# Attention and ResMLP on one Trainium2 core: the third product of the last group added straight from PSUM, one store moved to ScalarE's queue, and a new written order

## The chip, the cores and the metric

The kernel runs on one core of one Trainium2 chip. The core has five instruction streams: TensorE (matrix products; PE in the profile, its weight loads PEld), VectorE (DVE), ScalarE (ACT), GpSimd (POOL) and SyncE (SP), which here issues only DMAs; ScalarE and GpSimd issue some as well. The metric is the device time of one launch in microseconds, the median of several runs.

## The reference

```python
kv  = einsum('bhsd,bhse->bhde', k, v)          # 8 batches, 8 heads, 576 rows, 64 per head
o   = einsum('bhsd,bhde->bhse', q, kv)
x   = o / sqrt(mean(o*o, -1) + 1e-6) * g_norm  # then (b, s, h*d): 8 x 576 x 512
tok = einsum('ts,bsd->btd', w_tok, alpha1 * x + beta1)
u   = x + lam * tok
ch  = maximum((alpha2 * u + beta2) @ w_ch1, 0) @ w_ch2      # 512 -> 2048 -> 512
out = u + lam * ch
```

All inputs and the output are float32.

## The kernel before

The kernel is written for a planner. The class `Prog` records every operation (a group of matmuls with one purpose, one arithmetic instruction, or one DMA) with a number in the order of creation, and what it reads and writes. A string, `ORDER`, then lists all these numbers in one global sequence. Each engine executes its own operations in just that sequence; nothing is reordered on the chip. In the string `751:4+807:0` means that the matmuls of 751 and 807 are woven into each other, 751 taking PSUM bank 4 and 807 bank 0; an operation that opens a bank waits for all users of that bank's tile before. `GATES` adds waits that no data asks for: `632: 652` makes 632 wait for 652. `synchronize` turns all this into semaphores.

**The work.** Each batch has 576 rows: four blocks of 128 and a tail of 64. Tails of two batches share one tile of 128 rows, `xt[:, 0]` or `xt[:, 1]`. For each batch `kv` (line 638) multiplies k and v; ScalarE copies half of the result (`kvo`, L655), VectorE adds it to the other half (`kvc`, L657). `load_kv` loads k and v of the next batch on GpSimd's queue: 1 MB each (L1465) and a small tail each (L1469). `qt_steady` turns q: a VectorE transpose (L1475) and a ScalarE copy (L1478). `norm` (L729) multiplies q by kv and normalizes (L696 to L717; L714 and L712 are the last multiplications on VectorE). `tok` (L812) mixes the rows and VectorE adds the result (L822). `a2_dma` casts it on GpSimd (L900) and transposes it by DMA on SyncE's queue (L913) to `a2m`, the input of the channel MLP.

**Channel MLP.** The first product is `ch1` (L1090) with a ReLU on ScalarE (L919), for the last two batches `pairmm` (L1031, with the kept sums L1043) and `tailmm` (L972, ScalarE's copies L982). The second product is done in the Strassen-Winograd form by `strassen(b)`: seven `product`s (L1212) of half size in three PSUM banks `ta`, `tb` and `tc`. Weight and row sums are made by `both` on VectorE (L1174). A bank that goes on accumulating while one of its partial sums is needed elsewhere is treated by `keep`: ScalarE copies the bank to `tmp` (L1242), GpSimd adds `tmp` to the result (L1245). A finished sum is added by VectorE straight from PSUM, `last_add` (L1250). `store` then writes rows out (L1259 for tails, L1263 else; L1341 and L1345 are the stores of `finish`).

`strassen(NB)` is the last group: the tails of batches 4 to 7, one quarter of the usual size. Its operations from the third product on, with their numbers before:

| operation | engine | what |
|---|---|---|
| 1565 | VectorE | last add of batch 7, 128x512 |
| 1589, 1590 | TensorE | third product into `tc` |
| 1591, 1592 | ScalarE, GpSimd | `keep(tc, (dn, fh))`: copy and add |
| 1593, 1594 | TensorE | product into `ta` |
| 1595 | VectorE | `last_add(ta, dn, fh)`, on the same rows as 1592 |
| 1596, 1597 | SyncE, ScalarE | stores of those rows |
| 1598, 1599 | TensorE | product into `tc`, which goes on |
| 1600 | VectorE | `last_add(tc, up, fh)` |
| 1601, 1602 | SyncE, SyncE | stores of those rows |
| 1603, 1604 | TensorE | last product, into `ta` |
| 1605 | VectorE | `last_add(ta, dn, fl)` |
| 1606, 1607 | SyncE, ScalarE | stores of those rows |

Other numbers that come up below: 629, 639, 1146 (VectorE, adds and multiplications), 652, 1196 (VectorE, weight and row sums), 1199 (VectorE, last add of a batch), 1203 (GpSimd, `keep`'s add), 1234 and 1236 (VectorE, transposes of q) with the copy 1235 (ScalarE), 1277 (VectorE, L714), 633, 637, 645, 987, 991, 995, 999 (SyncE, transposes L913), 558, 564, 905, 917 (SyncE, stores), 743 to 746 (GpSimd's k and v loads; 743 and 745 the large, 744 and 746 the small ones), 716 (TensorE, product), 751 (TensorE, `norm`), 807 (TensorE, `ch1`), 1282 (TensorE, `tok`), 1331 (ScalarE, ReLU), 1344 and 1350 (ScalarE, kept sums), 1467 and 1475 (TensorE, `tailmm`), 1555, 1556, 1576, 1577, 1585 (TensorE, products).

Of the kernel before, what the change touches and what calls it, by code (L numbers as in the profile page):

```python
# [10 lines left out]
ACT = mybir.ActivationFunctionType  # L11
# [92 lines left out]
"""  # L104

GATES = {23: 52, 38: 67, 39: 73, 40: 163, 124: 151, 125: 213, 204: 196, 233: 269, 234: 216, 235:
# [7 lines left out]


class Op:


    __slots__ = ("tile", "q", "kind", "cost", "lat", "fns", "idx", "deps", "raw", "alloc", "tiles", "at",
                 "pos", "waits", "inc", "clock", "slot", "nbytes", "ns", "val", "form", "bias")  # L120

    def __init__(self, q, kind, cost, lat, fns, pri, idx):
        self.q, self.kind, self.cost, self.lat = q, kind, cost, lat
        self.fns, self.idx, self.bias = fns, idx, pri
        self.deps, self.raw = set(), set()
# [233 lines left out]
def bass_transnormer_attn__then__resmlp_affine_kernel(  # L359
# [15 lines left out]
    with ExitStack() as stack:  # L375
        P = Prog(nc, stack)
# [842 lines left out]
        def strassen(b):  # L1219
# [58 lines left out]
            if tails:  # L1278
                store(0, fl)
# [343 lines left out]
```

## Time and profile before

| what | value |
|---|---|
| median of 3 runs | 327.81 us (327.43 to 328.18) |
| the profiled execution | 328.12 us |
| its span, first to last instruction | 326.3 us |
| TensorE busy | 319.0 us, 98% |
| VectorE, ScalarE, GpSimd busy | 250.2, 177.1, 141.9 us |
| granted TensorE clock | 1.000 |

Times in rows of the profile are microseconds from the start of the span. A row of the timeline has the start, the duration, the engine, the line in the kernel, the operation, what it writes and reads, its shape and the number of instructions put together; in brackets stands how long the engine was idle before it and what ended the wait. A row of the waits has the total, the number and the longest. SPq and ACTq are DMA issues on the queues of SyncE and ScalarE; a DMA's landing is told apart from its issue. PEld are weight loads, which run ahead of the matmuls that use them.

### The profile page before, as it was taken

Reading aid. Unit: us, or ns where it says so; the run is one execution under the profiler, and the core shown is the slowest. Engines: PE = TensorE matmul, PEld = TensorE weight load, DVE = VectorE, ACT = ScalarE, POOL = GpSimd, SP = SyncE. Lnnn points to the kernel's source line nnn. Section 1 sums busy time; section 2 is a strip of 40 time slices with the busy share of each in tenths; the row PEclk is TensorE's granted clock in tenths of the full one; section 3 lists DMA queues with packets and bytes.
Section 4 is the critical chain, followed back from the end, with each engine's and each line's share of the span. In section 5 each row is a group of like instructions: output and inputs, shape, how many; then the busy total and the mean of one; then the engine's idle time right before and its main releaser. Section 6 shows DMA issues by size and latency. Waiting matters only on the chain.

```text
span 326.3 us, 6145 instructions
## 1 busy us (share of the span) xinstructions
PE 319.0 (98%) x2411; PEld 218.2 (67%) x2441; DVE 250.2 (77%) x459; ACT 177.1 (54%) x363; POOL 141.9 (43%) x147
## 2 busy tenths in 40 slices
PE   8989999999999999999999999999999999999996
PEld 7767664454766545786579874787657644589884
DVE  4586078667799997838985388889899899997672
ACT  5684572329633471738741876731883068765520
POOL 3699127798362562353337143455234600014041
PEclk9999999999999999999999999999999999999999
DMA  7999997999950994799449950998040340000116
GB/s 258 316 267 257 214 243 176 224 151 209 265 123 16 204 245 70 173 247 217 104 50 186 259 104 11 213 253 171 2 129 2 64 145 4 0 2 2 64 50 209
DMA packets 108532, 48.15 MB, mean 148 GB/s; under 512 B 82061, under 2 KB 101717, under 8 KB 108504
## 3 DMA queue, kind: packets, MB, share of 16 engines
q0 software_dynamic: 26800, 21.38, 33.4%
q1 hardware_dynamic: 72240, 25.06, 33.4%
q10 hardware_dynamic: 9464, 1.32, 2.5%
q8 instruction: 19, 0.31, 0.4%
q14 instruction: 9, 0.07, 0.1%
HBM read 38.82 MB, written 9.44 MB: 148 GB/s over the span
## 4 chain that ended last, share of the span: by engine, by line
PE 91%; DMA 3%; DVE 2%; ACT 1%; issue 1%; POOL 0%; ACTq 0%; SPq 0%
PE ps L1090 25%; PE ps L1212 25%; PE ps L1151 10%; PE ps L812 9%; PE ps L1031 7%; PE ps L729 3%; DMA hh<-in_moe_w_tok_dram 2%; PE ps L638 2%; PE ps L1104 2%; PE ps L972 2%; PE ps L857 1%; DMA xm<-in_q_dram 1%; PE ps L594 1%; PE ps L644 1%; PE ps L877 1%
## 5 line engine op out<-in xcount | busy, mean ns | idle before, releaser
L1090 PE MATMUL ps<-a2m,w 128*128 128x512 bf16 x370 | 96.1, 384 | 0.5 <-DMA a2m<-a2b 0.3
L717 POOL TENSOR_TENSOR rm<-xm,la_bc 128x512 bf16<-128x512 f32 x28 | 35.3, 1272 | 60.7 <-DVE xm L714 43.6
L1090 PEld LDWEIGHTS ps<-a2m,w 128*128 128x128 bf16 x384 | 36.2, 97 | 37.4 <-DMA a2m<-a2b 0.5
L919 ACT ACTIVATE hh<-ps,b 128x512 bf16<-128x512 f32 x72 | 47.5, 687 | 18.6 <-PE ps L1090 13.3
L1245 POOL TENSOR_TENSOR xm<-xm,tmp 128x512 f32<-128x512 f32 x18 | 22.8, 1270 | 63.5 <-DVE qp L1174 28.6
L729 PE MATMUL ps<-kvc,qt 128*128 128x128 f32 (+1 forms) x140 | 42.3, 403 | 0.1
L1212 PE MATMUL ps<-w,hh 128*128 128x256 bf16 x344 | 41.8, 273 | 0.1
L1212 PEld LDWEIGHTS ps<-w,hh 128*128 128x128 bf16 x344 | 33.4, 98 | 6.1 <-issue 0.4
L1151 PE MATMUL ps<-w,hh 128*128 128x512 bf16 x138 | 36.9, 385 | 0.1
L638 PE MATMUL ps<-vr,kr 128*128 128x128 f32 x112 | 34.7, 409 | 0.0
L699 DVE TENSOR_REDUCE small<-sq 128x8 f32<-128x512 f32 (+1 forms) x35 | 23.4, 675 | 11.7 <-ACT sq L696 11.6
L812 PE MATMUL ps<-rm,wt 128*128 128x512 bf16 x107 | 29.0, 381 | 0.3 <-DVE rtl L712 0.2
L1250 DVE TENSOR_TENSOR xm<-ps,xm 128x512 f32<-128x512 f32 x24 | 16.3, 687 | 16.5 <-POOL xm L1245 8.9
L729 PEld LDWEIGHTS ps<-kvc,qt 128*128 128x128 f32 (+1 forms) x140 | 27.2, 195 | 2.3 <-DVE kvc L657 0.7
L900 POOL CAST a2b<-xm 128x512 bf16<-128x512 f32 x24 | 14.3, 612 | 32.6 <-DVE xm L822 20.1
L1478 ACT ACTIVATE qt<-qp 128x576 fp32r<-128x576 f32 x24 | 16.0, 680 | 16.0 <-DVE qp L1475 16.0
L707 DVE TENSOR_TENSOR ps<-ps,small 128x512 f32<-128x512 f32 (+1 forms) x35 | 24.2, 694 | 0.6
L1242 ACT ACTIVATE tmp<-ps 128x512 f32<-128x512 f32 (+1 forms) x21 | 11.8, 566 | 23.5 <-PE ps L1212 23.4
L696 ACT ACTIVATE sq<-ps 128x512 f32<-128x512 f32 (+1 forms) x35 | 20.6, 596 | 6.7 <-PE ps L729 6.3
L919 ACT ACTIVATE hh<-ps 128x512 bf16<-128x512 f32 x32 | 17.5, 596 | 12.1 <-issue 7.4
L638 PEld LDWEIGHTS ps<-vr,kr 128*128 128x128 f32 x112 | 22.4, 200 | 1.5
L1151 PEld LDWEIGHTS ps<-w,hh 128*128 128x128 bf16 x144 | 13.4, 97 | 13.5 <-issue 0.4
(216 smaller groups left out, 616.8 us busy)
## 6 DMA issues: line engine op xcount, KB each, us to landing
out_dram<-xm SPq DMA_DIRECT2D x32, 256.0 KB, 2.4
kr<-in_k_dram POOLq DMA_DIRECT2D x7, 1024.0 KB, 8.0
vr<-in_v_dram POOLq DMA_DIRECT2D x7, 1024.0 KB, 8.2
qs<-in_q_dram SPq DMA_DIRECT2D x20, 288.0 KB, 4.4
w<-in_moe_w_ch_dram POOLq DMA_DIRECT2D x8, 512.0 KB, 10.9
xm<-in_q_dram SPq DMA_DIRECT2D x8, 288.0 KB, 5.8
qs<-in_v_dram SPq DMA_DIRECT2D x4, 288.0 KB, 5.7
w<-in_k_dram SPq DMA_DIRECT2D x4, 288.0 KB, 5.6
```

Source lines behind the costliest of these rows:

```text
L638: P.mm("fill", 128, [lambda e, t=t, c=c, h=h, o=128 * (h % 4): e.matmul(t.ap()[:, o:o + 128], kr4[:, h, c:c + 2, :].rearrange("p c d -> p ...
L699: P.op("DVE", dve(n), lambda e: e.tensor_reduce(out=st, in_=sq[rs, s3, 0:nst, :], axis=AX.X, op=ALU.add), r=[("sq", s3)], w=[("sm", s4)])
L707: P.op("DVE", dve(n), lambda e: e.tensor_tensor(out=grp(ps()), in0=grp(ps()), in1=st[..., None].to_broadcast([rs.stop - rs.start, nst, DH] ...
L717: P.op("POOL", pool(n), lambda e: e.tensor_tensor(out=r, in0=x.rearrange("p h e -> p (h e)"), in1=la, op=ALU.mult), r=xks + ["la"], w=rks)
L729: P.mm("fill", 128, [lambda e, p=p: e.matmul(dst(p), qt[:, p, cs], kvc[:, i, p, :], start=(p == 0), stop=(p == 3)) for p in range(4)], r=[ ...
L812: P.mm("fill", 512, [lambda e, sc=sc: e.matmul(t.ap(), wt[:, sc if sc < 4 else tw(b), 128 * c:128 * c + 128], rsrc(b, sc, al), start=(sc = ...
L919: P.op("ACT", act(512, 0 if f is None else 1), lambda e: e.activation(dst, t.ap(), ACT.Relu, bias=0.0 if f is None else b1[:, f:f + 1]), r ...
L1031: P.mm("main", 512, [lambda e, i=i: e.matmul(t.ap(), lhs[:, i, 128 * x + o:128 * x + o + 128], rhs[:, i, :], start=(first and i == 0), sto ...
L1090: P.mm("main", 512, [lambda e, dj=dj: e.matmul(t.ap(), w1[:, dj, 128 * fj:128 * fj + 128], a2m[:, b % 2, dj, :], start=(dj == 0), stop=(dj ...
L1151: P.mm("main", 512, [lambda e, fj=fj, t=t, c=c: e.matmul(t.ap(), (ht[:, fj, 128 * c:128 * c + 128] if c < 4 else hl[:, fj, :]), w2[:, fj, ...
L1212: P.mm("main", 256, [lambda e, c=c, fj=fj: e.matmul(t.ap()[:, 256 * c:256 * c + 256], at[:, fj, 128 * c:128 * c + 128], rhs(fj), start=(fi ...
L1245: P.op("POOL", pool(256 * n), lambda e, cs=cs, f=f: e.tensor_tensor(out=X[:, cs, f], in0=X[:, cs, f], in1=two(tmp[:, s]), op=ALU.add), r=x ...
```

## The change

Three things. In `strassen(NB)` the third product is no longer kept by a copy and an add, but added by VectorE with `last_add`; in batch groups before it `keep` stays. The store 1602 (rows 512 to 576 of batch 5, columns 256 to 512) is issued by ScalarE's queue with the semaphore `oz`. And `ORDER` is written anew from about 65 us on, with some changes in `GATES`; the work is the same, but on each engine many operations change places with a neighbour, and two banks differ (630: bank 7 for 6, 1286: bank 5 for 6). As 1592 falls away, numbers from 1593 on are one lower in the new string; 1591 is now VectorE's add.

```diff
     if tails:
         for i in range(2):
             bb = 4 + 2 * c + i
-            P.dma("ACT" if c and i else "SP", "oz" if c and i else "ot%d%d" % (c, i),
+            z = i and (c or f.start)
+            P.dma("ACT" if z else "SP", "oz" if z else "ot%d%d" % (c, i),
                   dcost(64, 43), lambda e, i=i, bb=bb: e.dma_start(
                       out[bb, 512:576, f], X[64 * i:64 * i + 64, c, f]),
...
     product(tc, True, A11, t1, lambda g: four(g, 0, 0, b) + [("t1", g)], False)
-    keep(tc, (dn, fh))
+    last_add(tc, dn, fh) if tails else keep(tc, (dn, fh))
     product(ta, False, A21, lambda j: B12[:, j, :],
```

The places of `ORDER` that are spoken of below, each cut out of its line:

```diff
- ... 727+630:6 728:4+634:3 690 653 631 729+638:7 635 691 652 639 629 684:6 730+642:5 ...
+ ... 727+630:7 728:4+634:3 653 690 631 729+638:7 635 691 639 629 652 684:6 730+642:5 ...
- 682:0 681 641 564 633 643 737 644 735 647 738 731 645 637 558 683 648 741 732 694:5 686:3 745 746 743 ...
+ 682:0 681 641 633 643 737 644 735 647 731 738 558 637 645 736 683 648 741 694:5 686:3 746 744 745 743 ...
- ... 710 713 711 714 712 716 751:4+807:0 715 717 721 ...
+ ... 710 713 711 714 712 751:4+807:0 716 715 717 721 ...
- ... 1088 1086 1000:4 917 995 905 900 991 997 1001 998 1002 1092 1090 987 999 1003 ...
+ ... 1088 1025 1086 1000:4 905 917 995 900 991 997 1001 998 1002 1092 1090 987 999 ...
- 1146 1231 1233 1224+1149:3 1143 1234 1225+1157:6 1150 1236 1235 ...
+ 1233 1224+1149:3 1143 1234 1146 1225+1157:6 1150 1236 1235 ...
- ... 1276 1196 1277 1206 1207 1278:1 1209 1282:3 1279 1199 1280 1203 ...
+ ... 1276 1199 1196 1277 1206 1207 1278:1 1209 1282:3 1279 1280 1203 ...
- ... 1321 1336 1325 1330 1331 1343 1349:4 1338:5 1344 1337 1305 1326 1339 1345 1350 1353:3 ...
+ ... 1321 1336 1325 1330 1343 1349:4 1338:5 1344 1337 1305 1326 1339 1345 1350 1331 1353:3 ...
- ... 1466 1518 1576:0 1467:6 1521 1540:7 1468 1469 1522 1470 1543 1471 1475 ...
+ ... 1466 1518 1514 1467:6 1540:7 1468 1469 1568 1576:0 1470 1471 1522 1543 1475 ...
- ... 1493 1570 1552 1494 1495 1571 1577 1553 1589:7 1555 1581 1580 1582 1554 1558 1556 1583 1557 1559 1585 ...
+ ... 1491 1490 1585 1492 1570 1555 1493 1571 1494 1529 1495 1556 1580 1531 1577 1557 ...
- 1564 1590 1565 1593 1591 1594 1592 1598 1599 1595 1597 1603 1567 1566 1596 1600 1604 1602 1605 1601 1607 1606
+ 1564 1590 1565 1592 1591 1593 1567 1597 1594 1566 1598 1596 1595 1602 1599 1603 1601 1600 1604 1606 1605
```

In `GATES` nine waits go and ten come:

```diff
- 456: 654, 878: 882, 1104: 1047, 1245: 1186, 1503: 1437, 1514: 1535, 1518: 1544, 1554: 1580, 1575: 1578
+ 878: 874, 1058: 1047, 1203: 1196, 1245: 1303, 1503: 1507, 1514: 1458, 1518: 1458, 1554: 1545, 1575: 1487, 1588: 1581
```

135 rows, old and new, of tables (GATES, ORDER) are left out of this document.

## The prediction

> **What bounds the kernel now.** I read the page first: the busy times, and then the chain that ended last.
>
> ```profile
> span 326.3 us, 6145 instructions
> ...
> PE 319.0 (98%) x2411; PEld 218.2 (67%) x2441; DVE 250.2 (77%) x459; ACT 177.1 (54%) x363; POOL 141.9 (43%) x147
> ...
> PE 91%; DMA 3%; DVE 2%; ACT 1%; issue 1%; POOL 0%; ACTq 0%; SPq 0%
> ...
> L1090 PEld LDWEIGHTS ps<-a2m,w 128*128 128x128 bf16 x384 | 36.2, 97 | 37.4 <-DMA a2m<-a2b 0.5
> L1212 PEld LDWEIGHTS ps<-w,hh 128*128 128x128 bf16 x344 | 33.4, 98 | 6.1 <-issue 0.4
> ```
>
> TensorE is busy for 98% and holds 91% of the chain. An operation taken from another engine is worth nothing by itself; only two things are: a wait of TensorE that goes, and the stretch after its last matmul. The last two rows tell what idle time is no wait: a weight load that follows a 512-column matmul has 37.4/384 = 0.10 us before it, one in the Strassen products (L1212) 6.1/344 = 0.02 us. What a load's idle has beyond that is lost time.
>
> Next the waits of the weight loads from 65 us on (the order before that is not touched). All are small, so the whole change can only be worth about 2 us:
>
> ```profile
> PEld ps L1090 <- DMA a2m<-a2b: 0.5, 2, 0.3
> ...
> PEld ps L1212 <- DVE xt L1250: 0.3, 1, 0.3
> PEld ps L812 <- DVE rtl L712: 0.3, 1, 0.3
> ```
>
> Last the timeline of the end, with the queues asked one by one:
>
> ```profile
> 319.86 0.69 DVE L1250 TENSOR_TENSOR xm<-ps,xm 128x512 f32<-128x512 f32 x1 [1.93 <-PE ps L1212]
> ...
> 320.30 0.38 ACT L1242 ACTIVATE tmp<-ps 128x256 f32<-128x256 f32 x1 [1.80 <-PE ps L1212]
> 320.76 0.72 POOL L1245 TENSOR_TENSOR xt<-xt,tmp 128x256 f32<-128x256 f32 x1 [1.46 <-ACT tmp L1242]
> 320.86 0.86 PEld L1212 LDWEIGHTS ps<-w,hh 128*128 128x128 bf16 x8
> 321.52 0.95 DVE L1250 TENSOR_TENSOR xt<-ps,xt 128x256 f32<-128x256 f32 x2 [0.96 <-POOL xt L1245]
> 321.99 0.77 PEld L1212 LDWEIGHTS ps<-ws,wt 128*128 128x128 bf16 x8 [0.27 <-DVE xt L1250]
> 323.08 0.42 DVE L1250 TENSOR_TENSOR xt<-ps,xt 128x256 f32<-128x256 f32 x1 [0.61 <-PE ps L1212]
> ```
> ```profile
> 322.50 0.59 SPq L1259 DMA_DIRECT2D out_dram<-xt  x1
> 323.77 0.59 SPq L1259 DMA_DIRECT2D out_dram<-xt  x1
> 323.54 0.47 ACTq L1259 DMA_DIRECT2D out_dram<-xt  x1
> DMA to landing us min/median/max: 1.9/2.0/2.2
> ```
>
> Here the reader sees the chain that the change aims at: ScalarE's copy of the third product, GpSimd's add (to 321.48), VectorE's add of `ta` (321.52 to 321.94), and only then the last product's weights at 321.99, 0.27 late. After the last add (323.08 + 0.42 = 323.50) ScalarE's store leaves at 323.54, SyncE's only at 323.77: that queue is still issuing the one before. 323.77 + 2.0 is the landing, and 0.5 us of closing steps complete the span.
>
> **The change, part by part** (numbers are those of `ORDER` before).
>
> *Third product.* Gone are ScalarE's copy 1591 (0.38) and GpSimd's add 1592 (0.72); neither engine has work behind them, so the removal is worth only what waited. Added is one 128x256 add on VectorE, 0.42 by the 323.08 row, behind add 1565 (319.86 to 320.55) and ahead of 1595. What is late next: product 1598 goes on in the same bank and now waits for this add; before it waited for the copy, done at 320.68, and had 0.18 to spare. The trace shows no such add right behind 1565. Nearest is the pair of L1250 adds below: 1.28 for two of 0.69, so the second starts 0.10 before the first ends; the other end is a start 0.03 after. The add then ends at 320.87 to 321.00, and 1598 is held by 0.06 to 0.19. I take 0.12, nearer the overlapped pair.
>
> ```profile
> 253.51 1.28 DVE L1250 TENSOR_TENSOR xm<-ps,xm 128x512 f32<-128x512 f32 x2
> ```
>
> [...]
>
> 1595 no longer needs GpSimd; it starts with its product's end (1594, some 0.9 before 1598's end) and is done before 1603 asks. The wait of 0.27 - 0.02 = 0.25 goes, 0.12 comes: **-0.13**.
>
> *Store.* Store 1602 moves from SyncE to ScalarE, sharing semaphore `oz` with 1597 and 1607. ScalarE's order becomes 1597, 1602, 1607, with no arithmetic behind them. Each issue is 0.47 to 0.59, and the last add ends 1.04 after 1600 does, so both queues are free when it ends, and both last stores leave 0.03 after it, as ScalarE's did, where SyncE's left at 323.77: **-0.24**. The issue is paid on ScalarE, hidden under the last product; if that cover were gone it would cost its 0.5.
>
> *New order of the other operations.* This is the larger part of the diff; five places touch a wait of TensorE.
>
> ```profile
> 202.37 1.23 SPq L913 DMA_TRANSPOSE a2m<-a2b  x1
> 203.64 1.05 SPq L1263 DMA_DIRECT2D out_dram<-xm  x2
> 204.73 2.55 SPq L913 DMA_TRANSPOSE a2m<-a2b  x2
> ...
> 206.80 0.91 POOL L1465 DMA_DIRECT2D vr<-in_v_dram  x1
> ...
> 215.16 0.54 PEld L1090 LDWEIGHTS ps<-a2m,w 128*128 128x128 bf16 x4 [0.32 <-DMA a2m<-a2b]
> ```
>
> (a) 215 us. Store 905 is one of the two in the 203.64 row, which stand among the transposes; it moves ahead of 917, into idle queue time. Transposes 991, 987 and 999 leave 0.5 us sooner, while only 0.30 (0.32 - 0.02) is missing: **-0.30**. Landing is bounded by not moving at all (0) and by the full wait.
>
> ```profile
> 228.96 0.68 ACT L1478 ACTIVATE qt<-qp 128x576 fp32r<-128x576 f32 x1 [0.57 <-DVE qp L1475]
> 230.22 0.68 ACT L1478 ACTIVATE qt<-qp 128x576 fp32r<-128x576 f32 x1 [0.57 <-DVE qp L1475]
> ...
> 232.44 0.43 DVE L657 TENSOR_TENSOR kvc<-ps,kvo 64x256 fp32r<-64x256 f32 x1 [0.69 <-ACT kvo L655]
> ...
> 233.23 0.19 PEld L729 LDWEIGHTS ps<-kvc,qt 128*128 128x128 f32 x1 [0.38 <-DVE kvc L657]
> ```
>
> (b) 233 us. VectorE's transpose 1234 goes ahead of add 1146, so ScalarE's copy 1235 (230.22) can start 0.57 sooner, right behind the copy before it (done at 229.64). The kvo copies behind it, which now run back to back with it, follow until they wait for their own product instead, and VectorE's kvc add follows them. Of those 0.57, half is needed: **-0.28** (0.38 - 0.10), bounds -0.28 and 0 (the product is late too).
>
> (c) 253 us. Add 1199 goes ahead of 1196 and 1277; 1277 frees the bank of `tok` 1282. 1277, below, ends at 252.87, and behind one more add, 0.5 to 0.7 with the overlap seen above, at 253.4 to 253.6; 1282 started at 253.34: **+0.07**, bounds 0 and 0.25.
>
> ```profile
> 252.18 0.69 DVE L714 TENSOR_TENSOR xt<-ps,g_bc 64x512 f32<-64x512 f32 x1
> 253.34 0.64 PEld L812 LDWEIGHTS ps<-rm,wt 128*128 128x128 bf16 x4
> ...
> 268.16 0.69 ACT L919 ACTIVATE hh<-ps,b 128x512 bf16<-128x512 f32 x1 [1.03 <-PE ps L1031]
> ...
> 270.06 0.16 PEld L1031 LDWEIGHTS ps<-qp,qs 128*128 128x128 bf16 x2 [0.27 <-ACT sq L1043]
> ```
>
> (d) 270 us. ScalarE's ReLU 1331 at 268.16 now goes behind the two kept sums (1344, 1350); without its 0.69 in front these can start sooner until their own products bound them, and 0.27 - 0.10 = **-0.17** is all that is needed; bounds -0.17 and 0.
>
> ```profile
> 303.28 0.39 PEld L972 LDWEIGHTS ps<-qs 128*128 128x128 bf16 x7 [0.19 <-ACT sq L982]
> ...
> 312.66 0.33 PEld L1212 LDWEIGHTS ps<-w,hh 128*128 128x128 bf16 x4 [0.19 <-ACT hh L982]
> ```
>
> (e) 303 and 312 us. 1467 goes ahead of 1576 (half a product, 0.43), so the four ScalarE copies that 1475 waits for start sooner; 1577 goes behind 1585, 1555 and 1556 (0.43 + 0.87 + 0.87), so that its input is needed 2.2 us later. Both waits go: 2 x (0.19 - 0.02) = **-0.34**.
>
> (f) 127 to 143 us, where it could cost. The casts of the next batch are gated on weight sum 652, which goes behind 639 and 629 (0.69 each): about 1.5 us later.
>
> ```profile
> 127.44 1.73 POOL L900 CAST a2b<-xm 128x512 bf16<-128x512 f32 x3 [6.45 <-DVE ws L1174]
> ...
> 133.40 0.95 POOL L1465 DMA_DIRECT2D vr<-in_v_dram  x1 [1.00 <-DMA a2m<-a2b]
> 134.34 0.69 POOL L1469 DMA_DIRECT2D vr<-in_v_dram  x1
> ...
> L913 SPq DMA_TRANSPOSE a2m<-a2b x4: 1190/1266/2070, 129.2 to 134.5; - x4
> DMA to landing us min/median/max: 3.3/4.2/8.2
> ```
>
> The last transpose left at 134.5 and landed 8.2 later, at 142.7, behind the 1 MB load of 133.40; there chunk product 807 took it with hardly a wait (0.2 of the first wait row above). Now store 564 leaves their run, 558 enters, and the last leaves between 134.5 and 136, say 135.3. But the small loads 746 and 744 (0.69 each) go ahead of the 1 MB load, which leaves near 133.4 + 1.5 + 1.4 = 136.3, after the transposes. With the median of 4.2 the last lands at 139.5; 807, whose unit goes ahead of 716 (half a product, 0.87), asks at about 141.7. I take **0**, bounds -0.2 and +3.1 (a landing after 9.4).
>
> The wait at 251 us on L712 stays: VectorE's operations ahead of it are the same ones, and its chain starts from TensorE's own product, so what was won earlier is carried through.
>
> Sum: -0.13 - 0.24 - 0.30 - 0.28 + 0.07 - 0.17 - 0.34 + 0 = **-1.4 us**. The profiled execution took 328.12 (span 326.3 and 1.8 around it); it would take 326.7. It lies 0.3 above the median of 327.81, so the forecast on the median is **326.4**.
>
> **Rivals.** *The waits change place.* The order wins at one place and loses at the next: VectorE, 77% busy over the span, is in the chain at each of them, and (a), (b) and (d) are given back to it. Only the end remains, -0.13 - 0.24 and part of (e): 327.1 to 327.6, about 327.4. For it: the list of many small waits, each a near tie. Against it: at each of them I found the next input ready by 0.1 us or more.
>
> *Transposes land late (slower).* At (f) the last chunk is later than 807 by as much as it then took: landing 9.4 after 135.3 is 144.7, 3.0 after 141.7. The total is -1.4 + 3.0 = +1.6: 329.4. It decides from a landing of about 8.5, where 2.1 is lost and the kernel is slower by over 0.2%; 8.2 was seen in this very place, behind a load that left a microsecond earlier than the last transpose. At 7.8 the gain is just cancelled: 327.8.
> [...]
>
> *The direct add holds 1598 longer than GpSimd's chain held 1603.* Then the first term is at worst +0.1 and the sum -1.2: 326.6, still the forecast's side.
>
> **How the numbers follow.** The forecast, with the third rival in it, gets 0.60, its own range 326.0 (all bounds good) to 327.1. Waits that change place get 0.20, late transposes 0.20, of which 0.15 beyond the point and 0.05 near a cancelled gain. One measurement here can tell about 0.2%, 0.66 us, from no change. So faster 0.60, same 0.25, slower 0.15. The range reaches to 327.9 and leaves out the slower case and little else.
>
> **What would show it.** Right: no ScalarE copy or GpSimd add after 319 us, three VectorE adds of 128x256 near 319.5, 320 and 321, the load of the last product's weights without idle before it, both queues' last stores at the same moment; no waits at 215, 233, 270, 303 and 312 us; the last matmul 1.1 to 1.2 us sooner. Wrong: a wait of L1090 on a2m above 0.3 us near 141 us, new waits of L729 or L812 on VectorE between 215 and 260, or a last store that still queues on SyncE.

## The result, and the profile after

The changed kernel takes 331.69 us (median, 329.63 to 332.92), the kernel before 328.03 on the same chip; the ratio is 1.0102, interval 1.0076 to 1.0129. The forecast was 326.4 with a range of 326.0 to 327.9: wrong in sign. Below, four slow executions are left out of the ratios, though not of the medians: 333.81 us of e2, 335.07 of e7, and 666 and 1171 of the kernel before beside e9 and e10. The profiled execution of the changed kernel took 332.92, the slowest of its six. Its page, the lines that answer to the first fence of the prediction (span, busy times, chain, the weight loads of L1091, which was L1090):

```profile
span 331.1 us, 6149 instructions
...
PE 322.1 (97%) x2411; PEld 220.3 (67%) x2441; DVE 251.3 (76%) x460; ACT 176.8 (53%) x362; POOL 140.1 (42%) x146
...
PE 88%; DVE 4%; DMA 3%; ACT 2%; SPq 1%; POOL 1%; issue 1%
...
L1091 PEld LDWEIGHTS ps<-a2m,w 128*128 128x128 bf16 x384 | 36.4, 98 | 40.8 <-DMA a2m<-a2b 3.4
```

The waits at `a2m` are 3.4 us instead of 0.5, but TensorE is also busy 3.1 us longer with the same 2411 matmuls. Two losses, then. The timeline of TensorE shows the place, (f) of the prediction:

```profile
144.68 0.10 PEld L1091 LDWEIGHTS ps<-a2m,w 128*128 128x128 bf16 x1 [3.35 <-DMA a2m<-a2b]
144.73 0.67 PE L730 MATMUL ps<-kvc,qt 128*128 128x128 f32 x1 [3.26 <-DMA a2m<-a2b]
```

The matmul of 144.73 takes 0.67, where the mean of its line is 0.40 in the page before (L729, 403 ns). The busy times by stretches of 1 us (time, length, busy us of PE, PEld, DVE, ACT, POOL with their instructions, then granted clock, DMA share, GB/s) show the clock beside it:

```profile
142.00:143.00 1.00, 0.00 (x0) 0.00 (x0) 0.62 (x1) 0.00 (x0) 0.00 (x0) 1.00 1.48 222
143.00:144.00 1.00, 0.00 (x0) 0.00 (x0) 0.00 (x0) 0.00 (x0) 0.00 (x0) 0.78 1.99 342
144.00:145.00 1.00, 0.27 (x1) 0.32 (x2) 0.00 (x0) 0.00 (x0) 0.00 (x0) 0.50 1.85 358
...
149.00:150.00 1.00, 1.00 (x7) 0.67 (x6) 0.00 (x0) 0.00 (x0) 0.00 (x0) 0.50 0.00 0
150.00:151.00 1.00, 1.00 (x9) 0.81 (x8) 0.58 (x1) 0.00 (x0) 0.00 (x0) 0.81 0.00 0
```

The granted clock falls to 0.50 while TensorE waits and stays there until 150.4; in the 5.7 us from the end of the wait to there 16 matmuls of L1213 take 3.62 us (146.76), where the 16 of 139.50 took 1.91. The fall is not in every execution: the two of the six with a mean granted clock of 0.999 took 329.63 and 330.88, the four with 0.990 to 0.995 took 331.33 to 332.92. GpSimd's loads and SyncE's transposes ahead of it, and the landing times of these four transposes:

```profile
133.64 0.74 POOL L1471 DMA_DIRECT2D vr<-in_v_dram  x1 [1.54 <-DMA a2m<-a2b]
134.37 0.70 POOL L1471 DMA_DIRECT2D kr<-in_k_dram  x1
135.03 0.93 POOL L1467 DMA_DIRECT2D vr<-in_v_dram  x1
```
```profile
130.53 3.02 SPq L914 DMA_TRANSPOSE a2m<-a2b  x2
133.59 0.59 SPq L1348 DMA_DIRECT2D out_dram<-xt  x1
134.23 2.61 SPq L914 DMA_TRANSPOSE a2m<-a2b  x2
```
```profile
L914 SPq DMA_TRANSPOSE a2m<-a2b x4: 1258/1286/1707, 130.5 to 135.6; - x4
...
DMA to landing us min/median/max: 2.5/3.3/9.1
```

The 1 MB load left at 135.03, the last transpose (645) at 135.6, half a microsecond behind it; it landed 9.1 later, while 637, sent at 134.23, ahead of the load, took 3.8.

To see the rest, the starts of the same TensorE operations are set against those of before, in the one profile of each run. The table gives the difference in us, the median over 6 us of the stream from the time named; what stands at 96 arises in the first 20 us, with the first loads (in the changed kernel it is -0.43 from 16 us on), and runs from -1.12 to +0.18.

```
us of before    96    126    150    198    216    240    258    318
changed       -0.43  -0.29  +5.65  +5.76  +5.56  +5.39  +5.48  +5.24
e1            -1.12  -1.09  -1.12  -0.99  -1.19  -1.37  -1.28  -1.52
e2            -0.30  +0.78  +1.27  +1.39  +1.19  +1.02  +1.11  +0.87
e3            -0.43  -0.41  -0.60  -0.48  -0.68  -0.85  -0.76  -1.00
e4            +0.08  +0.10  +3.92  +4.04  +4.32  +4.15  +4.24  +4.39
e5            -0.48  -0.46  +5.43  +5.55  +5.35  +5.17  +5.25  +5.01
e6            -0.40  -0.40  +2.48  +2.60  +2.40  +2.23  +2.31  +2.08
e7            +0.18  +0.93  +3.37  +3.37  +3.15  +3.15  +3.15  +3.15
e8            -0.54  -0.54  -0.73  -0.62  -0.82  -0.98  -0.89  -1.13
e9            -0.23  -0.21  -0.40  -0.36  -0.57  -0.73  -0.74  -0.98
```

Place (f) costs the changed kernel 5.65 + 0.29 = 5.94 us; all the rest from there to the last group wins 5.65 - 5.24 = 0.41. The tail after:

```profile
325.11 0.69 DVE L1251 TENSOR_TENSOR xm<-ps,xm 128x512 f32<-128x512 f32 x1 [1.93 <-PE ps L1213]
...
325.71 0.41 DVE L1251 TENSOR_TENSOR xt<-ps,xt 128x256 f32<-128x256 f32 x1
326.18 0.79 PEld L1213 LDWEIGHTS ps<-w,hh 128*128 128x128 bf16 x8
326.42 0.42 DVE L1251 TENSOR_TENSOR xt<-ps,xt 128x256 f32<-128x256 f32 x1 [0.29 <-PE ps L1213]
326.98 0.86 PEld L1213 LDWEIGHTS ps<-ws,wt 128*128 128x128 bf16 x8
328.16 0.42 DVE L1251 TENSOR_TENSOR xt<-ps,xt 128x256 f32<-128x256 f32 x1 [0.45 <-PE ps L1213]
328.62 0.47 SPq L1261 DMA_DIRECT2D out_dram<-xt  x1
328.62 0.51 ACTq L1261 DMA_DIRECT2D out_dram<-xt  x1
```

The third product's add now stands at 325.71 on VectorE; the last product's weights (326.98) have no idle before them, and both last stores leave at 328.62. The edits of the last group do what they say.

### The profile page after: what moved, and what is told of

Same layout as the page of the kernel before. It is cut to its first block, busy times and chain, and to the rows that moved or that the text cites. A ratio compares the mean times of both kernels' runs of the same rounds, so it can differ in the third digit from the quotient of the medians.

```text
span 331.1 us, 6149 instructions
## 1 busy us (share of the span) xinstructions
PE 322.1 (97%) x2411; PEld 220.3 (67%) x2441; DVE 251.3 (76%) x460; ACT 176.8 (53%) x362; POOL 140.1 (42%) x146
## 4 chain that ended last, share of the span: by engine, by line
PE 88%; DVE 4%; DMA 3%; ACT 2%; SPq 1%; POOL 1%; issue 1%
PE ps L1091 24%; PE ps L1213 22%; PE ps L1152 9%; PE ps L813 9%; PE ps L1032 7%; PE ps L730 3%; DMA a2m<-a2b 3%; PE ps L639 2%; PE ps L1105 2%; PE ps L973 2%; PE ps L466 1%; SPq L914 1%; PE ps L595 1%; PE ps L858 1%; DVE small L781 1%; PE ps L617 1%
## 5 line engine op out<-in xcount | busy, mean ns | idle before, releaser
L1091 PE MATMUL ps<-a2m,w 128*128 128x512 bf16 x369 | 96.8, 386 | 0.4 <-issue 0.2
L1091 PEld LDWEIGHTS ps<-a2m,w 128*128 128x128 bf16 x384 | 36.4, 98 | 40.8 <-DMA a2m<-a2b 3.4
L730 PE MATMUL ps<-kvc,qt 128*128 128x128 f32 (+1 forms) x140 | 43.2, 409 | 3.3 <-DMA a2m<-a2b 3.3
L1213 PE MATMUL ps<-w,hh 128*128 128x256 bf16 x344 | 43.9, 279 | 0.0
L1213 PEld LDWEIGHTS ps<-w,hh 128*128 128x128 bf16 x344 | 34.1, 100 | 7.1 <-issue 0.7
L1152 PEld LDWEIGHTS ps<-w,hh 128*128 128x128 bf16 x144 | 13.4, 97 | 13.4 <-issue 0.4
```

Source lines behind the costliest of these rows:

```text
L730: P.mm("fill", 128, [lambda e, p=p: e.matmul(dst(p), qt[:, p, cs], kvc[:, i, p, :], start=(p == 0), stop=(p == 3)) for p in range(4)], r=[ ...
L1091: P.mm("main", 512, [lambda e, dj=dj: e.matmul(t.ap(), w1[:, dj, 128 * fj:128 * fj + 128], a2m[:, b % 2, dj, :], start=(dj == 0), stop=(dj ...
L1152: P.mm("main", 512, [lambda e, fj=fj, t=t, c=c: e.matmul(t.ap(), (ht[:, fj, 128 * c:128 * c + 128] if c < 4 else hl[:, fj, :]), w2[:, fj, ...
L1213: P.mm("main", 256, [lambda e, c=c, fj=fj: e.matmul(t.ap()[:, 256 * c:256 * c + 256], at[:, fj, 128 * c:128 * c + 128], rhs(fj), start=(fi ...
```

## The experiments

The medians of the kernel before in the four comparisons are 328.03, 328.76 (e1 to e4), 328.31 (e5 to e8) and 328.10 us (e9 and e10), up to 0.2% apart, so each ratio is to the kernel before on the same chip.

**e1: place (f) as before.** In the changed kernel's order:

```diff
-635 691 639 629 652
+635 691 652 639 629
-641 633 643 737 644 735 647 731 738 558 637 645     (564 after 747)
+641 564 633 643 737 644 735 647 731 738 645 637 558
-746 744 745 743
+745 746 743                                          (744 after 697)
-751:4+807:0 716
+716 751:4+807:0
```

> The changed kernel with place (f) alone put back as it was before: weight sum 652 ahead of 639 and 629, store 564 among the transposes and store 558 behind them, the 1 MB load 745 ahead of the small loads, product 716 ahead of 751 and 807. Theory (late transposes): the wait of 3.3 us at 141 us goes and with it the low clock behind it, about 5.9 us together; what the rest of the change wins in the two traces (0.28 ahead of this place, 0.6 behind it) stays: about 327.2, below before. Rival (the new order loses at other places too, the wait only shows there): 328.5 or more.

326.95 us, ratio 0.9951 (0.9922 to 0.998): faster than before. The loss is all at this place. In its trace the wait is gone, and the table shows that the rest of the change wins 0.4 from 150 us to the last group, as in the changed kernel.

**e2: the load waits for the transpose.** `GATES` gets `745: 645`.

> The changed kernel with one more gate: the 1 MB load 745 waits for the landing of the last transpose 645. Theory (a transpose that leaves just behind the load lands with it): 645 leaves at 135.6 as before and lands 3.3 to 4.2 later, near 139.5, before it is asked for at 141.2; no wait, clock 1.00, about 327.0. Rival (the transposes are late because weight sum 652 delays the casts): casts and transposes leave as late as now, so the wait stays above 2 us and the time at 331 or more.

328.16, ratio 0.9991 (0.996 to 1.0022). Casts and transposes left as late as in the changed kernel or later (the last at 136.4, there 135.6), but the load left at 139.60, and the transpose landed 2.7 after it left. So a late cast alone does no harm; a transpose behind the load does. The kernel is 1.2 short of what was expected, and its trace shows two losses: at 111 us another transpose, 449, landed 5.6 after it left and TensorE lost 1.1 (this lies ahead of the gate, which cannot have caused it); and GpSimd, which issues the load, stood waiting for the landing for 3.7 us (to 139.60) with its adds of `keep` queued behind (141.38, in e3 138.06), so that VectorE's last adds came late and TensorE lost another 0.5 at 146 us.

**e3: weight sum 652 alone put back.**

```diff
-635 691 639 629 652
+635 691 652 639 629
```

> The changed kernel with weight sum 652 alone back ahead of 639 and 629. Theory (behind the load): casts, transposes and the load, which waits for a transpose, all leave 1.3 us sooner and keep their order, so the last transpose still lands about 9 after it left, near 143.3: a wait of about 2, and 328.5 to 330. Rival (the casts' delay is the whole cause): the wait goes, 327.0.

327.10, ratio 0.9972 (0.9944 to 1.0). The wait goes entirely, as the rival said; but not for the rival's reason, as e2 has shown. The load did not move with the casts by 1.3 us, as I had assumed, but by 0.6: what it waits for is a landing (641), and that came 0.6 sooner only. So the last transpose (134.02) now leaves 0.41 ahead of the load (134.43). Its landing times:

```profile
L914 SPq DMA_TRANSPOSE a2m<-a2b x4: 1195/1278/1969, 128.8 to 134.0; - x4
...
DMA to landing us min/median/max: 3.1/3.7/4.8
```

**e4: filler in the wait.** 54 matmuls of a constant tile ahead of 751 and 807, into the bank that 751 opens (`~54:4`; they wait for the bank's former users as 751 does):

```diff
-... 714 712 751:4+807:0 ...
+... 714 712 ~54:4 751:4+807:0 ...
```

> The changed kernel with 54 matmuls of no use (128x128, into the bank that 751 opens, 0.056 us each at full clock, 3.0 us) put into TensorE's stream ahead of 751 and 807. Theory (half of the loss is a clock that falls after an idle TensorE): the transposes land as late as now, but TensorE is busy, the granted clock stays 1.00, and some 2.6 us of the 5.9 come back: about 329.5. Rival (the clock falls for another reason, at that time whatever TensorE does): it falls to 0.50 as now, 332 or more.

332.87, ratio 1.0146 (1.0114 to 1.0178). The clock stays at 1.00 in the profile and at 0.999 or more in all four executions, and the place costs 3.82 instead of 5.94; but the whole is no faster, and 3.4 us over what was expected. The filler (54 x 0.056 = 3.0 us, an estimate from the spacing of the 128x128 matmuls of L972 in the trace before) stands in the stream of every execution, also where the wait would be shorter, and in this trace a wait came at 215 us that the changed kernel does not have (a transpose landing 9.0 after it left). Without the changed kernel on the same chip this settles nothing; hence e5 and e6.

**e5 and e6: the changed kernel again, and with 18 fillers in place of 54.**

> The changed kernel as it is, on the chip of the three kernels beside it, as their measure. Theory: again about 1% above before, with a wait of 2.5 to 3.5 us at 141 to 145 us and a low granted clock behind it in most executions. Rival (a matter of the first chip): within 0.3% of before.

333.37, ratio 1.0155 (1.0116 to 1.0194): the loss is there beside these kernels too, with the clock at 0.50 from 143.5 to 150.3 again.

> The changed kernel with 18 useless matmuls (1.0 us) ahead of 751 and 807 instead of 54. The idle stretch of TensorE that is left is about 2.3 us. Theory (the clock falls after about 2.1 us of idle: in the changed kernel TensorE stops at 141.5 and the clock is below 1 from the microsecond 143 to 144 on): the profile stands at the edge; if the stretch is under 2.1 the clock stays 1.00 and the time is 2 to 2.6 us below that of the changed kernel, over it the same time. Rival (the low clock costs little, since e4 was no faster in its median): the same time whether it falls or not.

330.66, ratio 1.0093 (1.0058 to 1.0128), 2.7 under e5 on the same chip. In the trace the wait is 2.0 behind 1.0 of filler, as long in all as e5's 3.2, and the clock does not fall:

```profile
142.00:143.00 1.00, 0.42 (x7) 0.27 (x4) 0.51 (x1) 0.00 (x0) 0.00 (x0) 1.00 1.49 300
143.00:144.00 1.00, 0.00 (x0) 0.00 (x0) 0.00 (x0) 0.00 (x0) 0.00 (x0) 1.00 1.66 382
144.00:145.00 1.00, 0.73 (x6) 0.56 (x6) 0.00 (x0) 0.00 (x0) 0.00 (x0) 1.00 1.84 382
```

Place (f) then costs 2.88 (0.40 + 2.48) instead of 5.94 in the changed kernel and 5.89 in e5: about 3 us are waiting, about 3 us the low clock. The traces show it by taking the one away and leaving the other. The filler does not keep the clock up in every execution: five with a mean of 0.999 or 1.000 took 329.76 to 331.02, three with 0.995 took 331.77 to 334.54.

**e7: 652 alone moved, in the kernel before.**

```diff
-635 691 652 639 629
+635 691 639 629 652
```

> The kernel before with one change: weight sum 652 goes behind 639 and 629. Theory (a transpose that leaves behind the 1 MB load lands with it): casts and transposes leave 1.3 us later; the load 745 waits for the first landing and hardly moves (133.4 to 134), so the last transpose, 637, leaves 2 us behind the load and lands 8 to 10 later, at 143.5 to 145.5, for a product that asks at 142.5: a wait of 1 to 3 us, 329 to 332. Rival (652 alone does no harm, the store and the small loads moved with it do): within 0.2% of before.

331.59, ratio 1.0098 (1.0066 to 1.013): one operation put two places back makes the kernel before slower by 3.3 us. The whole change costs 5.1 on the same chip (e5); the clock stays at 1.00 in e7's profile, so this is a wait without the fall behind it.

```profile
PEld ps L1090 <- DMA a2m<-a2b: 2.6, 1, 2.6
PEld ps L1090 <- DVE small L705: 1.1, 1, 1.1
```
```profile
L913 SPq DMA_TRANSPOSE a2m<-a2b x4: 1201/1486/1718, 131.8 to 136.7; - x4
...
DMA to landing us min/median/max: 2.5/5.7/9.3
```

The first wait is the expected one: the last transpose left 1.8 behind the load and landed 9.3 later. The second stands at 112 us and is put down to VectorE; the input that came last there is transpose 449, which landed 5.1 after it left, 0.06 before its product. It lies ahead of the moved operation, so it is no effect of it: place (f) costs e7 2.44 (3.37 - 0.93) in the table, and the 0.75 ahead of it is this execution's own.

**e8: 652 back, and the loads at 107 us back.**

```diff
-635 691 639 629 652
+635 691 652 639 629
-... 530 531 594 526 529 521 614:7+555 582 585 584
+... 530 531 594 526 529 521 614:7+555 585 584 582
```

> The changed kernel with two operations put back: weight sum 652 ahead of 639 and 629, and at 107 us the 1 MB load 582 behind the small load 585 and the load 584. Theory: the last transpose at 141 us lands 2 us early (as in the run with 652 alone), and the one at 111 us, which landed 0.06 to 0.3 us before its product asked, gets back the 0.7 us that it had before; no late landing is left, the executions spread less, and the time is 0.3 to 0.6% under before, at or a little under the run with 652 alone. Rival (the spread of the runs has another source): same spread and time as with 652 alone.

327.15, ratio 0.9962 (0.9938 to 0.9986). Transpose 449 lands 1.02 before its product, in the runs with the changed order of the loads 0.06 to 0.44 (0.70 in the kernel before); but in e9, which has e8's order here, it is 0.14, and in e7, which has that of before, 0.06. The spread is 1.9 us (326.18 to 328.09) against e3's 2.6, on another chip. That the loads at 107 us matter is not shown.

**e9: e8, and two places put back where the new order lost.** 916 behind 964 and 1199 behind 1279.

> The kernel of e8 with two more operations put back where the traces show that the new order lost: VectorE's add 916 behind 962 and 964 (ahead of them it stood waiting for its product, and the 196 us wait of the row mixing on L712 followed, 0.1 us), and the last add 1199 behind 1277 (the 252 us wait, 0.1 us). Theory: both waits go in the trace, 0.2 us, and the rest stays: 326.9 on a chip where e8 takes 327.15, which is less than the times can tell apart. Rival (the waits go and come back at the next place): the last matmul stands where it does in e8.

326.62, ratio 0.9954 (0.9939 to 0.9969): the lowest time of all, on another chip than e1, whose ratio of 0.9951 is as good. Both waits went and did not come back: from 150 us to the last group it wins 0.58 where e8 wins 0.40. Only the trace can tell that; the times of e8 and e9 cannot.

**e10: the two edits of the last group alone, in the kernel before.** The code of the change, and its order behind 1564.

> The kernel before with the two edits of the last group alone: the direct add of the third product and the store on ScalarE's queue, with the order of the changed kernel behind operation 1564 only. Theory: the last product's weights come 0.16 sooner against the rest of the stream (0.07 of waiting in front of 1598 comes, 0.25 in front of 1603 goes), and the last landing another 0.09 sooner, since two stores that leave together take 1.95 and 2.2: 0.25 us in all, under what the times can show. Rival of the forecast (0.13 and 0.24): 0.37 in all.

328.09, ratio 1.0005 (0.998 to 1.0029): no difference that the times show. In the trace the start of 1604 gains 0.17 on the stream before it, the last landing another 0.09.

## Why the prediction was wrong

**The step that failed is (f).** The casts' delay (1.34 us in the trace, 1.5 forecast) and the last transpose's start (135.58, forecast 135.3) were right. Wrong was the sentence that the load "leaves near 133.4 + 1.5 + 1.4 = 136.3, after the transposes". I let the load move with the casts. It waits for the landing of the first transpose, and that transpose, later, landed 2.8 after it left where before it took 3.9. All twelve traces split so: 2.4 to 3.1 with 652 behind 639 and 629, 3.9 to 4.1 with 652 ahead of them; why is not shown. The small loads started at 133.64, 0.24 later than the large one had, and the large one left at 135.03 instead of 136.3. Ahead of the transpose by 0.55 us instead of behind it by 1: with that sign the median of 4.2 had nothing to say, and the 8.2 of the same row, taken behind the load, was the one to use.

The sign separates the landings of the twelve traces. Start of the last transpose less start of the load 745, and from start to landing, in us:

```
e2     -3.18   2.7        changed  +0.55   9.1
e3     -0.41   4.8        e5       +0.53   9.3
e8     -0.41   6.4        e6       +0.54   8.7
e9     -0.41   6.6        e4       +0.55   9.4
                          e1       +0.92   8.0
                          before   +1.07   8.2
                          e10      +1.07   7.8
                          e7       +1.81   9.3
```

Behind the load it lands within 2 us of the load's own landing in all eight traces (144.64 and 144.85 in the changed kernel, 142.62 and 141.56 before). Ahead of it the gain is less sure: three traces with the same lead of 0.41 spread from 4.8 to 6.6. A pair of the same kind stands at 215 us, transpose 999 and the next 1 MB load. In three traces (before, e7, e10) 999 leaves 0.5 behind that load and lands 7.5 to 7.8 later. In nine it leaves 0.2 ahead: eight land 5.4 to 6.9 later, but e4 9.0. So a lead of 0.2 us makes the long landing rare here and does not rule it out.

So the last transpose took 2.7 us where the load left 3.18 behind it (e2), 4.8 to 6.6 with the load 0.41 behind it, and 7.8 to 9.4 behind the load. Why one that leaves half a microsecond behind the load lands together with it is not shown.

**The rival was priced too low.** It had the landing of 9.1 (9.4 forecast) and the sign, and stood at 329.4. The wait is 3.35, close to its 3.0; the other 3 us is the low clock, which appeared in no term: in the trace before TensorE is idle for 0.48 us at most (7.2 us from the start), and the clock is 1.00 throughout.

**The gains were there, but half as large.** The sizes come from the table, the places from the rows below:

```profile
202.21 0.33 PEld L813 LDWEIGHTS ps<-rm,wt 128*128 128x128 bf16 x3 [0.20 <-DVE rtl L713]
...
220.63 0.64 PEld L1091 LDWEIGHTS ps<-a2m,w 128*128 128x128 bf16 x4
...
238.53 0.19 PEld L730 LDWEIGHTS ps<-kvc,qt 128*128 128x128 f32 x1
...
258.92 0.55 PEld L813 LDWEIGHTS ps<-rm,wt 128*128 128x128 bf16 x4 [0.20 <-DVE xt L715]
```

Third product, forecast -0.13: -0.16. The direct add starts 0.09 before the add ahead of it ends (325.71; 325.11 + 0.69), so the overlap that the prediction took from a row holds here too. The wait of 0.25 is gone. The hold before 1598 is 0.07 (I took 0.12), but only in the weight load: the next load and the matmuls are on time again, so it costs nothing. That -0.16 came near -0.13 is luck: the wait was priced too high and the hold too.

This is the second step that failed: the sum took a weight load's idle time for lost time. Loads run ahead of their matmuls (the load of 326.98 in the tail above by 0.11), and part of a load's wait does not reach the matmuls. Where a wait goes, the first load comes 0.26 (third product), 0.30 (a) and 0.26 (b) sooner, and at the very next load 0.09 of it is lost again.

Store, forecast -0.24: -0.08. Both last stores leave 0.03 after the add, as said. But the two that leave together at 328.62 land after 1.94 (SyncE's) and 2.19 (ScalarE's); before they left apart by 0.23 and took 2.04 and 1.93. I had counted the issue and let the landing be. The profile before had such a pair already: stores 1596 and 1597 left together at 321.97 and took 1.96 and 2.22.

(a) 215 us, forecast -0.30: -0.20. The wait is gone and the last transpose (999) lands 2.8 early. Most of the change is the landing itself: 999 now leaves 0.22 ahead of the load and lands 5.7 later, where it left 0.53 behind and took 7.8. That sign was not in the sum; here it turned the right way, by luck.

(b) 233 us, forecast -0.28: -0.17. The load at 238.53 has no marked wait left.

(c) 253 us, forecast +0.07: +0.09, as said: the last row waits 0.20 for L715.

(d) 270 us, forecast -0.17: 0. The wait shrank at one product and came back at the next.

(e) 303 and 312 us, forecast -0.34: -0.24.

Not forecast: +0.1 at 196 us (the first row: 202.21 there). VectorE's add 916 went ahead of 962, waited for its product, and the chain to L713 behind it came late; e9 took it away.

The sum of these is about -0.7 instead of -1.4; e1, e3, e8 and e9 show a gain in their times, 0.3 to 0.5% under before (e3's interval reaches 1.0). That is more than 0.7 us, and the rest is not settled: e1's trace and the one of before differ by 0.4 between 150 us and the last group. The kernel before spreads from 327.0 to 331.7 in the comparisons, its products at 142 and 215 us start 0.04 after the landing that they wait for, so that they feel every change of it, and a profile shows one execution only.

## What to carry to other kernels

When operations change places, ask of each DMA not how much later it leaves but whom it now follows: the same transpose took 4.8 to 6.6 us to its landing 0.4 ahead of a 1 MB load and 8.7 to 9.4 half a microsecond behind it, and the order of two queues can flip when both are moved by different releases (here a cast and a landing). A wait that is "just covered" in the profile before is the first place to look at, and the price of a miss can be more than the wait (here about 3 us of waiting and about 3 us at a clock of 0.50). Edits that win tenths in a trace are read from the trace, aligned by operation; the times could not show the two edits that the change is named for.

## What was not expected of the hardware

In the changed kernel the granted clock fell to 0.50 at 143.6, 2.1 us after TensorE had stopped (141.5), and came back at 150.4, 6.8 us later; in e5 at 143.5 and 150.3. The idle stretches were 3.3 and 3.1 us. In e7 TensorE stood still for 2.46 us, and the clock stayed at 1.00:

```profile
144.00:145.00 1.00, 0.00 (x0) 0.00 (x0) 0.63 (x1) 0.00 (x0) 0.34 (x1) 1.00 1.37 290
145.00:146.00 1.00, 0.00 (x0) 0.00 (x0) 0.06 (x1) 0.00 (x0) 0.00 (x0) 1.00 1.36 354
```

So the 2.1 us of idle that stood in e6's theory do not settle it: in the profiles the clock fell in the idle stretches of 3.3 and 3.1 us and stayed at 1.00 in those of 2.46 (e7) and 1.85 (e6). Executions of one kernel differ too: the mean granted clock is 0.990 to 0.999 in the six of the changed kernel, 0.995 to 1.000 in e6's eight and 0.990 to 1.000 in e7's ten. What decides whether it falls is not shown.

The other is the last transpose of a group beside the 1 MB load of another queue: at 135 us 2.7 to 6.6 us from start to landing ahead of the load and 7.8 to 9.4 behind it, at 215 us 5.4 to 9.0 and 7.5 to 7.8.
